# Scores of two chunks back to back in steps 3 to 5, x of step 3 transposed by TensorE, and the last output rows in two column parts

## The chip, the core and the metric

The kernel runs on one core of one Trainium2 chip. The metric is device time in microseconds (us) from launch to end, lower is better. Before the change the median of 5 runs is 200.76 us (200.41 to 204.0).

## What is computed

Gated linear attention over 4 batches, 8 heads, 768 positions and head dimension 48, followed by a feed-forward block with a ReLU gate on the 3072 resulting rows of 384 columns:

```python
f = sigmoid(f_logit)
for t in range(S):
    state = f[:, :, t, :, None] * state + k[:, :, t] outer v[:, :, t]
    y[:, :, t] = q[:, :, t] @ state
x = y.transpose(0, 2, 1, 3).reshape(B * S, H * D)
out = (relu(x @ w_gate) * (x @ w_val)) @ w_out      # 384 -> 1536 -> 384
```

Inputs and output are float32; the kernel multiplies in bfloat16 and accumulates in float32.

## The kernel before

The sequence is cut into 6 steps (`c` = 0 to 5) of 128 positions. In each step there is one *chunk* per batch (`b` = 0 to 3), so 24 chunks, numbered `w = c * 4 + b`. For a chunk, ScalarE turns the forget gate into logarithms, TensorE adds them up over the positions (L580) and ScalarE makes the factors `expo` from them (L589, L591). GpSimd multiplies k and q with these factors into `hats` (L600, L603) and casts v into `vpad` (L556). The transposed q and k are in `qkT`: in steps 1 and 2 TensorE transposes them (L613, the copy at L619), from step 3 on a DMA through the transposing crossbar does it (L622, issued by SyncE). *Scores* are k·q for every pair of positions in the chunk, for 8 heads: eight matmuls (L636) with only 48 of the array's 128 rows in use, alternating between rows 0 to 47 and rows 64 to 111, into two PSUM banks `sA` and `sB`. VectorE multiplies each bank with the causal mask into `ptm` (L642). Then TensorE makes y from the old state (L671) and from `ptm` and `vpad` (L675), ScalarE copies y to `xn` (L689), and `xn` is transposed into `xT`: by TensorE and a VectorE copy (L697, L701) while `c < first_xbar_x`, else by a crossbar DMA issued by SyncE (L705). For the next step, TensorE multiplies `hats` with `vpad` (L716), VectorE adds the old state (L730), GpSimd multiplies with the decay (L732).

The feed-forward block of a step follows its chunks: `ffn_hidden` makes, for each of 12 blocks of 128 hidden columns, a gate product and a value product, three matmuls each (L748), ReLU on ScalarE (L755), gate times value on VectorE into `gT` (L759). Steps 0 and 1 do so for two chunks at a time (256 columns), the later ones for all four (512 columns). `ffn_out` multiplies `gT` with `w_out`, 12 matmuls of 384 columns for each chunk (L770), ScalarE copies the rows to `osb` (L782), SyncE stores them (L785). The output products of one step are spread over the hidden products of the next.

All instructions are recorded first and then put in order by a small planner, `Plan`: each has an engine, what it reads and writes, an assumed duration `occ`, a latency `lat` and a priority. The planner gives each engine one fixed order; at run time every engine works through its order and waits on semaphores. So a changed duration or limit moves instructions all over the kernel. PSUM has 8 banks, which the planner hands out; `Plan`'s limits say how many each kind of tile may hold: here `s` (scores) 2, `f` (feed-forward) 4, and 1 each for `y`, `kv`, `bc`, `tp` (a transposed tile) and `w`. Loads, crossbar transposes and stores are all issued by SyncE, in one fixed order; a load of step `c + 1` or later (L397) also waits until the load three before it has landed. The weights are loaded from GpSimd's queue (L417). Until the first hidden product of step 0 TensorE is kept running by matmuls on zeros (L453), which the planner drops from there on.

The last rows stored are those of chunk 3 of step 5: 12 matmuls, one copy, one store.

Of the kernel before, what the change touches and what calls it, by code (L numbers as in the profile page):

```python
# [5 lines left out]
AF = mybir.ActivationFunctionType  # L6
# [37 lines left out]
class Plan:  # L44
# [184 lines left out]
def bass_hgrn2_outer__then__ffn_reglu_kernel(  # L229
# [21 lines left out]
    spread_engines = ['ACT', 'DVE', 'ACT', 'ACT']  # L251
    load_engine = 'SP'
    n_tiled = 1
    first_xbar_x = 3
    load_batches = 2
    hat_engines = ['DVE', 'POOL']
    groups = [(0,0,4,1),(1,0,2,0),(1,2,4,0),(2,0,4,0),(3,0,4,0),(4,0,4,0),(5,0,4,0)]
    B, H, S, D = q.shape
    C = 128
    NC = S // C  # L260
    HD = H * D
    DM, DFF = w_gate.shape
    NK = HD // 128
    NJ = DFF // 128
# [11 lines left out]
    bneg = [sb(f"bneg{i}", [128, 2, H, 64], BF16) for i in range(NB)]  # L276
# [5 lines left out]
    qkT_all = sb("qkT", [128, NQ, 2, NP, C], BF16)  # L282
    qkT = [qkT_all[:, i, :, :, :] for i in range(NQ)]
    NM = 3
    ptm = [sb(f"ptm{i}", [128, 2, NP, C], BF16) for i in range(NM)]
    NV = 4
    vpad = [sb(f"vpad{i}", [128, VW], BF16) for i in range(NV)]
# [18 lines left out]
    osb = [sb(f"osb{i}", [128, DM], F32) for i in range(NO)]  # L306
    tri = sb("tri", [128, C], BF16)
# [4 lines left out]
    zeros = sb("zeros", [128, 256], BF16)  # L312
    ident = sb("ident", [128, 128], BF16)
    ones = sb("ones", [128, 1], BF16)
    banks = [nc.alloc_psum_tensor(f"ps{i}", [128, 512], F32) for i in range(8)]

    pl = Plan({"bc": 1, "tp": 1, "s": 2, "y": 1, "kv": 1, "f": 4, "w": 1})
    pl.settled, pl.margin = 40.0, {"PE": 0.5, "SP": 0.6}
    add = pl.add
    gp, ve, sc, te, sy = nc.gpsimd, nc.vector, nc.scalar, nc.tensor, nc.sync  # L320

    def pe_t(*cols):
        return sum(max(n, 64) / 2400.0 + 0.0025 for n in cols)

    PE_L = 0.30

    def act_t(n):
        return dict(occ=0.06 + n / 1200.0, lat=0.25)
# [24 lines left out]
        ["ident"], ["ident"], occ=0.3, prio=-8)  # L353
    add("POOL", lambda: gp.memset(ones[:], 1.0), [], ["ones"], occ=0.1, prio=-8)

    def zero(eng, e, t, name, cols, prio):
        add(eng, lambda: e.memzero(t), [], [name], occ=0.15 + cols / 2000.0, prio=prio)  # L357

    zero("DVE", ve, zeros[:], "zeros", 128, -20)
    for i in range(NB):  # L360
        zero("DVE", ve, bneg[i][:], f"bneg{i}", 1024, -9)
    for i in range(NH):
# [41 lines left out]
    WJ = NJ // wsteps  # L404
# [21 lines left out]
    for item in early:  # L426
# [17 lines left out]
    def chain(line, *args, **kw):  # L444

        last = tails.get(line)
        tails[line] = add(*args, follows=[last] if last else [], **kw)
        return tails[line]
# [3 lines left out]
    for i in range(NWARM):  # L452
        op = add("PE", lambda: te.matmul(cold.ap[:, 0:256], zeros[:, 0:128], zeros[:, :]), ["zeros"], [cold], occ=0.22 if i < 17 else 0.11,  # L453
                 lat=PE_L, prio=1000000, opens=[cold] if i == 0 else [])
# [3 lines left out]
    def first_pair(pr):  # L458
        P = pr * 20
        bs = (2 * pr, 2 * pr + 1)  # L460
# [83 lines left out]
    def attention(c, b):  # L544
        w = c * B + b
        P = w * 10
        li = c % NL
        bi, bj = (w // 2) % NB, w % 2
        ei, hi, qi, mi, vi, ai = w % NE, w % NH, w % NQ, w % NM, w % NV, w % NA
        xi = c % NX  # L550
        fin, kin, qin, vin = (ld[n][li] for n in "fkqv")

        qk_key = [f"qkT{qi}_0", f"qkT{qi}_1"]
# [3 lines left out]
            prio=P + 3, occ=0.15 + HD / 1200.0 * 1.1, lat=0.2)  # L557
# [7 lines left out]
        else:  # L565
            parts = [(b, b + 2)] if b % 2 == 0 else []
# [9 lines left out]
            bn = bneg[bi][:, bj, :, :]  # L576
            bc = Bank("bc")

            def cum():
# [2 lines left out]
                    mm = te.matmul(bc.ap[:, HD + p:HD + p + 1],  # L582
                                   bn[:, 2 * p:2 * p + 2, :].rearrange("p h d -> p (h d)"), ones[:, :])
                return mm
            chain("cum", "PE", cum, ["tri", "ones", f"bneg{bi}", f"bn{bi}_{bj}"], [bc], occ=0.48, lat=PE_L,
                prio=P, opens=[bc])

            ex = expo[ei]
# [17 lines left out]
            if c < first_xbar_qk:  # L606
                tp = Bank("tp")

                def transposes():
# [7 lines left out]
                    opens=[tp])  # L617
# [12 lines left out]
        sA, sB = Bank("s"), Bank("s")  # L630

        def scores():
# [3 lines left out]
                    mm = te.matmul(s.ap[:, p * C:(p + 1) * C], qkT[qi][lo:lo + D, 1, p, :],  # L636
                                   qkT[qi][lo:lo + D, 0, p, :])
            return mm
        chain("scores", "PE", scores, qk_key, [sA, sB], occ=0.36, lat=PE_L, prio=P + 5, opens=[sA, sB])
        mask = tri[:].unsqueeze(1).to_broadcast([128, NP, C])  # L640
        for j, s in ((0, sA), (1, sB)):
            add("DVE", lambda j=j, s=s: ve.tensor_tensor(  # L642
# [3 lines left out]
        y = Bank("y")  # L646
# [38 lines left out]
        else:  # L685
# [5 lines left out]
            if c < first_xbar_x:  # L691
# [3 lines left out]
                def transpose_x():  # L695
                    for kt in range(NK):
# [3 lines left out]
                      opens=[xp])  # L700
# [3 lines left out]
            else:  # L704
                op = add("SP", lambda: sy.dma_start(xT[xi][:, :, b * C:(b + 1) * C], xn[ni][:, :], transpose=True),  # L705
                         [f"xn{ni}"], x_key, prio=P + 8, occ=1.2, lat=1.2)
# [3 lines left out]
        if c < NC - 1:  # L710
            kv = Bank("kv")
            s_new = st[b][c % 2]

            def state():
# [6 lines left out]
                occ=pe_t(96, 96, 96, 96), lat=PE_L, prio=P + 6 if c else 50 + b, opens=[kv])  # L721
# [6 lines left out]
            else:  # L728
# [3 lines left out]
                add("POOL", lambda: gp.tensor_tensor(t4(s_new), t4(tmp), rate, ALU.mult),  # L732
                    [key] + dk, [f"S{b}_{c % 2}"], prio=P + 8, **pool_t(HD))


    def ffn_hidden(c, b0, b1, j):
        xi, gi, ri = c % NX, c % NG, (count["h"]) % NR
# [24 lines left out]
    def ffn_out(g, *bs):  # L762

        gi = g % NG
        outs = [Bank("f") for b in bs]

        def proj_out(o, b, s):
            def run():
                for j in range(s * OJ, (s + 1) * OJ):
                    mm = te.matmul(o.ap[:, 0:DM], gT[gi][:, j, b * C:(b + 1) * C], wo[:, j, :],  # L770
                                   start=(j == 0), stop=(j == NJ - 1))
                return mm
            return run
        for s in range(NJ // OJ):
            js = range(s * OJ, (s + 1) * OJ)
            for o, b in zip(outs, bs):
                P = (g + 1) * B * 10 + 5 + NJ * 3 + b * 3
                chain("ffn", "PE", proj_out(o, b, s), [f"gT{gi}_{j}_{b}" for j in js] + sorted({f"wo{j // WJ}" for j in js}),
                      [o], occ=pe_t(*[DM] * OJ), lat=PE_L, prio=P + 1000, opens=[o] if s == 0 else [])
        for o, b in zip(outs, bs):  # L780
            oi, P = (g * B + b) % NO, (g + 1) * B * 10 + 5 + NJ * 3 + b * 3
            add("ACT", lambda o=o, oi=oi: sc.activation(osb[oi][:, :], o.ap[:, 0:DM], AF.Copy), [o], [f"osb{oi}"],  # L782
                prio=P, **act_t(DM))
            dst = bass.AP(tensor=out.tensor, offset=(b * S + g * C) * DM, ap=[[DM, C], [1, DM]])
            op = add("SP", lambda dst=dst, oi=oi: sy.dma_start(dst, osb[oi][:, :]), [f"osb{oi}"], [f"out{g}_{b}"],  # L785
                     occ=0.2, lat=0.9, prio=P)
            dma(op, f"osb{oi}", 0.45)

    OJ = 4
    OPAIR = 2  # L790
# [5 lines left out]
    for c in range(NC):  # L796
        for b in range(0, B, load_batches):
            for n in "fkqv":
                if c > max(int(x.split(".")[0]) for x in sent):
                    if load_engine == "SP":  # L800
                        loads.append(load(n, c, b, b + load_batches, loads[-flight:][:1]))
                    else:
                        loads.append(load(n, c, b, b + load_batches, paced=loads[-flight:][:1], eng="ACT"))
        for b in range(B):
            attention(c, b)
        if c == 0 and split_first:
            for s in range(wsteps):
                for b0 in (0, 2):
                    for j in range(s * WJ, (s + 1) * WJ):
                        ffn_hidden(0, b0, b0 + 2, j)  # L810
            for b in range(0, B, OPAIR):
                ffn_out(0, *range(b, b + OPAIR))
        for gc, b0, b1, now in groups:
            if gc != c or (c == 0 and split_first):
                continue
            for j in range(NJ):
                ffn_hidden(c, b0, b1, j)
                if pend and (NJ - 1 - j) * 1.0 / NJ * len0 < len(pend):
                    ffn_out(*pend.pop(0))
# [11 lines left out]
    for e in ("PE", "ACT", "DVE", "POOL"):  # L831
        n = 0
# [72 lines left out]
```

## Time and profile before

| | |
|---|---|
| median of 5 runs | 200.76 us |
| the profiled execution | 200.41 us, of which the span of the instructions is 198.7 us |
| VectorE / ScalarE / GpSimd busy | 107.3 / 115.1 / 77.2 us of the span |
| TensorE clock granted | full speed throughout |
| matmuls of the feed-forward block (L748, L770) | 125.0 and 52.2 us by the page |
| scores (L636) | 192 matmuls in 24 groups of 8 |
| crossbar transposes of x (L705) | 12, of which 4 in step 3 |

TensorE's row in the page is its matmul time; matmuls overlap each other in the pipeline, so the duration of one (say 326 ns) is longer than the time after which the next one starts. Where the text speaks of a *cadence*, it is the time from one group's start to the next group's start in the timeline, divided by the matmuls in the group.

### The profile page before, as it was taken

Reading aid. Unit: us, or ns where it says so; the run is one execution under the profiler, and the core shown is the slowest. Engines: PE = TensorE matmul, PEld = TensorE weight load, DVE = VectorE, ACT = ScalarE, POOL = GpSimd, SP = SyncE. Lnnn points to the kernel's source line nnn. Section 1 sums busy time; section 2 is a strip of 40 time slices with the busy share of each in tenths; the row PEclk is TensorE's granted clock in tenths of the full one; section 3 lists DMA queues with packets and bytes.
Section 4 is the critical chain, followed back from the end, with each engine's and each line's share of the span. In section 5 each row is a group of like instructions: output and inputs, shape, how many; then the busy total and the mean of one; then the engine's idle time right before and its main releaser. Section 6 shows DMA issues by size and latency. Waiting matters only on the chain.

```text
span 198.7 us, 4530 instructions
## 1 busy us (share of the span) xinstructions
PE 192.1 (97%) x1796; PEld 122.8 (62%) x1796; DVE 107.3 (54%) x208; ACT 115.1 (58%) x263; POOL 77.2 (39%) x111
## 2 busy tenths in 40 slices
PE   7999999999999999999998979999999999999994
PEld 5877688856888787755553535555555555544552
DVE  7268865564399877648737443636265233443300
ACT  2786767906788587876759466386425334344311
POOL 5198303823859677693564174504500000000000
PEclk9999999999999999999999999999999999999999
DMA  5999999999999999999997899989942200111112
GB/s 122 236 226 206 188 212 191 205 206 242 262 200 230 187 241 217 147 228 216 159 193 158 175 186 202 206 189 185 182 112 59 63 35 5 40 40 43 40 71 87
DMA packets 118180, 31.74 MB, mean 160 GB/s; under 512 B 111248, under 2 KB 118160, under 8 KB 118160
## 3 DMA queue, kind: packets, MB, share of 16 engines
q1 hardware_dynamic: 114176, 27.93, 71.4%
q0 software_dynamic: 3984, 3.54, 11.2%
q8 instruction: 14, 0.23, 0.5%
q14 instruction: 6, 0.05, 0.1%
HBM read 25.95 MB, written 4.72 MB: 154 GB/s over the span
## 4 chain that ended last, share of the span: by engine, by line
PE 67%; DMA 17%; SPq 9%; ACT 3%; POOL 2%; issue 1%
PE ps L748 35%; PE ps L770 21%; DMA v_in<-in_v_dram 9%; SPq L397 8%; DMA wv<-in_moe_w_val_dram 3%; PE ps L636 3%; DMA q_in<-in_q_dram 3%; DMA f_in<-in_f_logit_dram 2%; PE ps L675 2%; PE ps L613 2%; PE ps L671 1%; PE ps L716 1%; ACT relu L755 1%; PE ps L580 1%; POOL hats L603 1%; POOL vpad L556 1%
## 5 line engine op out<-in xcount | busy, mean ns | idle before, releaser
L759 DVE TENSOR_TENSOR gT<-relu,ps 128x256 bf16<-128x256 bf16 (+1 forms) x96 | 52.2, 552 | 58.4 <-PE ps L748 40.2
L748 PE MATMUL ps<-xT,wv 128*128 128x256 bf16 (+1 forms) x288 | 62.5, 326 | 0.2 <-DMA wv<-in_moe_w_val_dram 0.2
L748 PE MATMUL ps<-xT,wg 128*128 128x256 bf16 (+1 forms) x288 | 62.5, 326 | 0.1
L755 ACT ACTIVATE relu<-ps 128x256 bf16<-128x256 f32 (+1 forms) x96 | 46.0, 489 | 27.2 <-PE ps L748 26.9
L770 PE MATMUL ps<-wo,gT 128*128 128x384 bf16 x288 | 52.2, 326 | 0.0
L770 PEld LDWEIGHTS ps<-wo,gT 128*128 128x128 bf16 x288 | 26.6, 97 | 16.8
L748 PEld LDWEIGHTS ps<-xT,wv 128*128 128x128 bf16 x288 | 26.1, 97 | 16.4 <-DMA wv<-in_moe_w_val_dram 0.4
L642 DVE TENSOR_TENSOR ptm<-ps,tri 128x512 bf16<-128x512 f32 x48 | 31.0, 685 | 9.5 <-PE ps L636 9.4
L748 PEld LDWEIGHTS ps<-xT,wg 128*128 128x128 bf16 x288 | 26.6, 98 | 15.1 <-DMA xT<-xn 0.8
L782 ACT ACTIVATE osb<-ps 128x384 f32<-128x384 f32 x24 | 11.7, 491 | 32.4 <-PE ps L770 32.4
L600 POOL TENSOR_TENSOR hats<-k_in,expo 128x384 bf16<-128x384 f32 x20 | 20.0, 998 | 17.1 <-ACT expo L589 17.1
L603 POOL TENSOR_TENSOR hats<-q_in,expo 128x384 bf16<-128x384 f32 x20 | 19.8, 998 | 11.0 <-DMA q_in<-in_q_dram 9.7
L732 POOL TENSOR_TENSOR st<-ssum,dec 128x384 bf16<-128x384 f32 x16 | 13.2, 828 | 12.9 <-DVE ssum L730 12.9
L453 PE MATMUL ps<-zeros 128*128 128x256 bf16 x96 | 14.1, 305 | 1.1 <-DVE zeros L357 1.1
L556 POOL CAST vpad<-v_in 128x384 bf16<-128x384 f32 x24 | 12.2, 524 | 4.7 <-DMA v_in<-in_v_dram 4.7
L689 ACT ACTIVATE xn<-ps 128x384 bf16<-128x384 f32 x20 | 9.8, 490 | 6.0 <-PE ps L675 6.0
L589 ACT ACTIVATE expo<-ps 128x384 f32<-128x384 f32 x20 | 9.8, 490 | 3.9 <-PE ps L582 3.7
L453 PEld LDWEIGHTS ps<-zeros 128*128 128x128 bf16 x96 | 10.0, 109 | 3.1 <-DVE zeros L357 1.1
L570 ACT ACTIVATE f_in<-f_in 128x768 f32<-128x768 f32 x10 | 8.4, 838 | 4.3 <-DMA f_in<-in_f_logit_dram 4.3
L730 DVE TENSOR_TENSOR ssum<-ps,st 128x384 f32<-128x384 f32 x16 | 8.8, 552 | 3.5 <-PE ps L716 3.5
L636 PE MATMUL ps<-qkT 48*128 48x128 bf16 x192 | 9.5, 219 | 0.5 <-DMA qkT<-hats 0.5
L591 ACT ACTIVATE expo<-ps 128x384 f32<-128x384 f32 x20 | 9.9, 495 | 0.0
(71 smaller groups left out, 153.8 us busy)
## 6 DMA issues: line engine op xcount, KB each, us to landing
out_dram<-osb SPq DMA_DIRECT2D x24, 192.0 KB, 2.2
f_in<-in_f_logit_dram SPq DMA_DIRECT2D x10, 384.0 KB, 5.7
k_in<-in_k_dram SPq DMA_DIRECT2D x10, 384.0 KB, 5.4
q_in<-in_q_dram SPq DMA_DIRECT2D x10, 384.0 KB, 5.1
v_in<-in_v_dram SPq DMA_DIRECT2D x10, 384.0 KB, 5.2
wg<-in_moe_w_gate_dram POOLq DMA_DIRECT2D x3, 384.0 KB, 7.1
wv<-in_moe_w_val_dram POOLq DMA_DIRECT2D x3, 384.0 KB, 7.0
wo<-in_moe_w_out_dram POOLq DMA_DIRECT2D x3, 384.0 KB, 7.3
```

What stands on the lines that cost most here:

```text
L397: op = add(eng, lambda: e.dma_start(dst, src), [], [f"{n}{c % NL}_{b}" for b in range(b0, b1)], occ=(0.8 if eng == "SP" else 0.3) * (b1 - ...
L453: op = add("PE", lambda: te.matmul(cold.ap[:, 0:256], zeros[:, 0:128], zeros[:, :]), ["zeros"], [cold], occ=0.22 if i < 17 else 0.11, lat= ...
L556: add("POOL", lambda: gp.tensor_copy(vout, vin[:, b, :, :].rearrange("p (n j) d -> p n j d", j=2)), [f"v{li}_{b}", f"vpad{vi}"], [f"v_{vi} ...
L600: add("POOL", lambda: gp.tensor_tensor(hk, kin[:, b, :, :], ex[:, 1, :].rearrange("p (h d) -> p h d", h=H), ALU.mult), [f"k{li}_{b}", f"ex ...
L603: add("POOL", lambda: gp.tensor_tensor(hq, qin[:, b, :, :], ex[:, 0, :].rearrange("p (h d) -> p h d", h=H), ALU.mult), [f"q{li}_{b}", f"ex ...
L636: mm = te.matmul(s.ap[:, p * C:(p + 1) * C], qkT[qi][lo:lo + D, 1, p, :], qkT[qi][lo:lo + D, 0, p, :])
L642: add("DVE", lambda j=j, s=s: ve.tensor_tensor(ptm[mi][:, j, :, :], s.ap[:, :].rearrange("p (n t) -> p n t", n=NP), mask, ALU.mult), [s, " ...
L732: add("POOL", lambda: gp.tensor_tensor(t4(s_new), t4(tmp), rate, ALU.mult), [key] + dk, [f"S{b}_{c % 2}"], prio=P + 8, **pool_t(HD))
L748: mm = te.matmul(bank.ap[:, 0:n], wt[:, kt, j * 128:(j + 1) * 128], xT[xi][:, kt, n0:n1], start=(kt == 0), stop=(kt == NK - 1))
L755: add("ACT", lambda: sc.activation(relu[ri][:, 0:n], gate.ap[:, 0:n], AF.Relu), [gate], [f"relu{ri}"], prio=P, **act_t(n))
L759: add("DVE", lambda: ve.tensor_tensor(gT[gi][:, j, n0:n1], relu[ri][:, 0:n], val.ap[:, 0:n], ALU.mult), [val, f"relu{ri}"], [f"gT{gi}_{j}_ ...
L770: mm = te.matmul(o.ap[:, 0:DM], gT[gi][:, j, b * C:(b + 1) * C], wo[:, j, :], start=(j == 0), stop=(j == NJ - 1))
```

## The change

Four things are edited, and the planner then makes a new order for every engine:

- In steps 3 to 5 (`PAIR`) the chunks are handled two at a time by a new function `attend`: the scores of both chunks are one entry in TensorE's order, 16 matmuls, which opens four PSUM banks at once. The limit of `s` goes from 2 to 4, for all steps.
- `first_xbar_x` goes from 3 to 4: x of step 3 is transposed by TensorE and copied by VectorE; the four crossbar transposes of that step are no longer issued.
- The last chunk's output rows are made, copied and stored as columns 0 to 255 and columns 256 to 383, one part after the other, each with its own PSUM bank.
- Two assumed times of the planner: a sum over positions in steps 1 to 5 counts 0.29 us in place of 0.48, and the clearing of `zeros` gets a latency of 0.9 us.

```diff
-    first_xbar_x = 3
+    first_xbar_x = 4
+    TAIL = [0, 256, 384]
+    PAIR = [1, 1, 1, 2, 2, 2]
-    pl = Plan({"bc": 1, "tp": 1, "s": 2, "y": 1, "kv": 1, "f": 4, "w": 1})
+    pl = Plan({"bc": 1, "tp": 1, "s": 4, "y": 1, "kv": 1, "f": 4, "w": 1})
...
-    zero("DVE", ve, zeros[:], "zeros", 128, -20)
+    zero("DVE", ve, zeros[:], "zeros", 128, -20, 0.9)
...
-            chain("cum", "PE", cum, [...], [bc], occ=0.48, lat=PE_L,
+            chain("cum", "PE", cum, [...], [bc], occ=0.29, lat=PE_L,
...
-        chain("scores", "PE", scores, qk_key, [sA, sB], occ=0.36, lat=PE_L, prio=P + 5, opens=[sA, sB])
+        yield P, qk_key, scores, [sA, sB]
...
+    def attend(c, bs):
+        works = [attention(c, b) for b in bs]
+        heads = [next(x) for x in works]
+        def scores():
+            for h in heads:
+                mm = h[2]()
+            return mm
+        sbanks = [x for h in heads for x in h[3]]
+        chain("scores", "PE", scores, [x for h in heads for x in h[1]], sbanks, occ=0.2 + 0.22 * len(heads), lat=PE_L,
+              prio=heads[0][0] + 5, opens=sbanks)
+        for x in works:
+            for _ in x:
+                pass
...
-        for b in range(B):
-            attention(c, b)
+        n = PAIR[c]
+        for b in range(0, B, n):
+            attend(c, range(b, b + n))
...
     def ffn_out(g, *bs):
-        outs = [Bank("f") for b in bs]
+        cuts = TAIL if (g, bs[-1]) == (NC - 1, B - 1) else [0, DM]
+        parts = [(b, n0, n1, Bank("f")) for b in bs for n0, n1 in zip(cuts, cuts[1:])]
...
-                    mm = te.matmul(o.ap[:, 0:DM], gT[gi][:, j, b * C:(b + 1) * C], wo[:, j, :],
+                    mm = te.matmul(o.ap[:, 0:n1 - n0], gT[gi][:, j, b * C:(b + 1) * C], wo[:, j, n0:n1],
...
+        if len(cuts) > 2:
+            for part in parts:
+                for s in range(NJ // OJ):
+                    rows(*part, s)
```

In the new order TensorE has these differences that the next part needs. Up to the multiplication for the next state of the first chunk of step 1 (the first one of L716 with `hats`) it stands 12 output products behind the 48 hidden ones, and not 16. In step 0 the fourth transposition of `hats` and the scores and back-transpositions of chunks 2 and 3 all stand before the first value product; before, the scores of chunk 3 stood behind it. On SyncE, the loads of f and k for the second half of step 4 stand before the crossbar transposes of that step's first chunk, the q load directly behind the first of these, the v load behind the second.

More of the change, by code (lines that the diff above doesn't have):

```diff
@@ L354, in bass_hgrn2_outer__then__ffn_reglu_kernel, with zero @@
     add("POOL", lambda: gp.memset(ones[:], 1.0), [], ["ones"], occ=0.1, prio=-8)
-    def zero(eng, e, t, name, cols, prio):
-        add(eng, lambda: e.memzero(t), [], [name], occ=0.15 + cols / 2000.0, prio=prio)
-    zero("DVE", ve, zeros[:], "zeros", 128, -20)
+    def zero(eng, e, t, name, cols, prio, lat=0.2):
+        add(eng, lambda: e.memzero(t), [], [name], occ=0.15 + cols / 2000.0, lat=lat, prio=prio)
+    zero("DVE", ve, zeros[:], "zeros", 128, -20, 0.9)
     for i in range(NB):
@@ L584, in cum @@
                 return mm
-            chain("cum", "PE", cum, ["tri", "ones", f"bneg{bi}", f"bn{bi}_{bj}"], [bc], occ=0.48, lat=PE_L,
+            chain("cum", "PE", cum, ["tri", "ones", f"bneg{bi}", f"bn{bi}_{bj}"], [bc], occ=0.29, lat=PE_L,
                 prio=P, opens=[bc])
@@ L764, in ffn_out, with proj_out @@
         gi = g % NG
-        outs = [Bank("f") for b in bs]
-        def proj_out(o, b, s):
+        cuts = TAIL if (g, bs[-1]) == (NC - 1, B - 1) else [0, DM]
+        parts = [(b, n0, n1, Bank("f")) for b in bs for n0, n1 in zip(cuts, cuts[1:])]
+        def proj_out(o, b, s, n0, n1):
             def run():
                 for j in range(s * OJ, (s + 1) * OJ):
-                    mm = te.matmul(o.ap[:, 0:DM], gT[gi][:, j, b * C:(b + 1) * C], wo[:, j, :],
+                    mm = te.matmul(o.ap[:, 0:n1 - n0], gT[gi][:, j, b * C:(b + 1) * C], wo[:, j, n0:n1],
                                    start=(j == 0), stop=(j == NJ - 1))
@@ L773, in proj_out, with rows @@
             return run
-        for s in range(NJ // OJ):
+        def rows(b, n0, n1, o, s):
             js = range(s * OJ, (s + 1) * OJ)
[L776 to L780, printed above, removed]
+            P = (g + 1) * B * 10 + 5 + NJ * 3 + b * 3
+            chain("ffn", "PE", proj_out(o, b, s, n0, n1), [f"gT{gi}_{j}_{b}" for j in js] + sorted({f"wo{j // WJ}" for j in js}),
+                  [o], occ=pe_t(*[n1 - n0] * OJ), lat=PE_L, prio=P + 1000, opens=[o] if s == 0 else [])
+        if len(cuts) > 2:
+            for part in parts:
+                for s in range(NJ // OJ):
+                    rows(*part, s)
+        else:
+            for s in range(NJ // OJ):
+                for part in parts:
+                    rows(*part, s)
+        for b, n0, n1, o in parts:
             oi, P = (g * B + b) % NO, (g + 1) * B * 10 + 5 + NJ * 3 + b * 3
[L782 to L785, printed above, removed]
+            add("ACT", lambda o=o, oi=oi, n0=n0, n1=n1: sc.activation(osb[oi][:, n0:n1], o.ap[:, 0:n1 - n0], AF.Copy), [o], [f"osb{oi}_{x}" for x in TAIL[:-1] if n0 <= x < n1],
+                prio=P, **act_t(n1 - n0))
+            dst = bass.AP(tensor=out.tensor, offset=(b * S + g * C) * DM + n0, ap=[[DM, C], [1, n1 - n0]])
+            op = add("SP", lambda dst=dst, oi=oi, n0=n0, n1=n1: sy.dma_start(dst, osb[oi][:, n0:n1]), [f"osb{oi}_{x}" for x in TAIL[:-1] if n0 <= x < n1], [f"out{g}_{b}_{n0}"],
                      occ=0.2, lat=0.9, prio=P)
-            dma(op, f"osb{oi}", 0.45)
+            dma(op, f"osb{oi}_{n0}", 0.45 * (n1 - n0) / DM)
     OJ = 4
```

## The prediction

> **What bounds the kernel now.** I read the page's busy shares first, then TensorE's waits, then its timeline around each wait, then SyncE's timeline there.
>
> ```profile
> PE 192.1 (97%) x1796; PEld 122.8 (62%) x1796; DVE 107.3 (54%) x208; ACT 115.1 (58%) x263; POOL 77.2 (39%) x111
> ```
>
> TensorE is busy for 192.1 of 198.7 us; no other engine passes 58%. So there are only two ways to gain: less TensorE time, or fewer of its stalls. Its own waits:
>
> ```profile
> PE ps L716 <- POOL vpad L556: 1.6, 2, 1.1
> PE ps L453 <- DVE zeros L357: 1.1, 1, 1.1
> PE ps L636 <- DMA qkT<-hats: 0.5, 1, 0.5
> PE ps L580 <- ACT bneg L573: 0.2, 1, 0.2
> PE ps L748 <- DMA wv<-in_moe_w_val_dram: 0.2, 1, 0.2
> ```
>
> None is for a PSUM bank. L716 waits twice: 0.48 us at 43.88 and 1.11 us at 115.94. The first ends with a landing: v of step 1, issued at 31.39, lands at 43.27, is cast, and L716 starts at 43.88. Nothing in TensorE's order moves that moment, so I call it **the pin** and count work from there. The second, in the chain of waits:
>
> ```profile
> 107.87 0.37 SPq L705
> 108.24 0.05 issue
> 108.29 5.14 DMA q_in<-in_q_dram
> 113.43 0.07 issue
> 113.50 1.95 POOL hats L603 x2
> 115.44 0.46 POOL vpad L556
> ```
>
> A load of q for step 4 is issued only at 108.29, behind a crossbar transpose of x of step 3 (L705), and GpSimd and TensorE wait for it. The same happens ten microseconds earlier: the f load leaves at 98.38, behind a transpose that held SyncE from 95.38 to 98.34, and the wait on bneg at 105.35 follows. **SyncE's queue is what makes the late stalls.**
>
> Cadences in the timeline show more than the waits: where a group took longer from start to next start than its like does elsewhere. L748 x3 (512 columns) takes 0.65; at 114.03 it took 1.92 (+1.27), at 107.62 before scores 1.27 in place of 0.74 (+0.53), at 104.34 1.01 (+0.37), at 138.34 0.81 (+0.17); scores at 108.90 took 0.49 in place of 0.33 (+0.16). Sum 2.50 us, all between 104 and 139.
>
> **Scores in pairs.** The timeline around one group:
>
> ```profile
> 122.01 0.81 PE L748 MATMUL ps<-xT,wv 128*128 128x512 bf16 x3
> 122.66 0.81 PE L748 MATMUL ps<-xT,wg 128*128 128x512 bf16 x3
> 123.40 0.40 PE L636 MATMUL ps<-qkT 48*128 48x128 bf16 x8
> 123.73 0.61 PE L748 MATMUL ps<-xT,wv 128*128 128x512 bf16 x2
> ```
>
> From 122.66 to 123.40 is 0.74, not 0.65: 0.09 on entering the 48-row form. The eight then take 0.33. They run in pairs (the starts lie at 0, 66, 122 and 177 ns), one pair each 0.056, which is also the cadence of a 128-column transpose (L613, 8 in 0.446). So four pairs need 0.22 and 0.11 goes on leaving. One group costs 0.42, two 0.84. Sixteen in a row do not occur in this trace: between no gain (0.84) and one entry and exit (0.09 + 8 x 0.056 + 0.11 = 0.65). I take 0.65, since pairs inside a group show no such cost. Six times 0.20 saved: **-1.19 us**, between 0 and -1.2. The price is banks: four of eight are held until VectorE has done four maskings (L642, 0.685 each: 2.74 us) where it was 1.37. The Trainium skill warns of just this (TensorEngine Tiling (Array Packing), "Gotcha 1: PSUM Pressure" and "PSUM Bottleneck": row tiles need banks of their own, and emptying PSUM may become the bound). By that rule the pair would hand its gain back; by the rows VectorE is busy 14.3 of 30 us between 120 and 150, and no wait on a bank shows. I go by the rows and keep the rule for a rival.
>
> **x of step 3 on TensorE.** Added are 4 x 3 transposes. L697's cadence is 0.166 for 3, next to feed-forward matmuls without a switching cost: 4 x 0.166 = **+0.67**. The Trainium skill prices a TensorE transpose at about 275 ns in a kernel (TensorE: Matmul & The Clock Gate, "Part 4: PE-mode transpose"), which gives 3.3 us and would make this edit a loss. The row has 219 ns for one from start to end, but 56 ns to the next start, and it is the next start that a full TensorE pays; the rule's figure is a latency. I take 0.67. Four copies of 0.352 (L701) go to VectorE, +1.4 us beside 16 idle us between 80 and 120: nothing on the path; uncovered they would cost 0.35 each at the first hidden product of step 4. ScalarE's copies to xn (L689) stay.
>
> Removed from SyncE are four transposes, at 92.40 (2.31), 95.38 (2.96), 103.74 (1.25) and 106.99 (1.25), 7.8 us of its queue with their waits on xn. What stood behind them moves up. f and k of step 4's second half go before the transposes of its first chunk, which start when `hats` is done (98.65); q follows at about 101 (a transpose holds the queue for 1.3 to 3.5), and with the 5.1 us of that load lands at 106. TensorE reaches L716 of that chunk at about 111 in the new order. Before it GpSimd needs two q products, one k product and the cast, 1.0 + 1.0 + 1.0 + 0.5 = 3.5: ready at 109.5. Slack some 1.5 us where there was a wait of 1.1. So the 2.50 should go. Next late would be the second crossbar transpose of a chunk pair, for a pair of scores now waits for both; by the same reckoning it lands at about 105 to 106 against scores at 109. New waits of the fresh order I allow **0.4**, between 0 and 2: among them the start of step 2, where a transposition, the multiplication for the next state, x and scores stand with only one hidden product between, and the 0.685 copy at L619 may come 0.2 late. Together **-2.1**.
>
> **The start.** In step 0 more stands before the first value product: transposition (0.45), ScalarE's two spreads (0.68 each, L526), then scores. In place of 21.71 (the landing of wv) I put it at about 22.8. The new order has 4 output products fewer before the pin (4 x 0.1625 = 0.65), and there were 0.48 of waiting: it still arrives at about 43.4, the pin stays at 43.9. But those four products come after it: **+0.65**. Bounds: if v lands earlier, up to -0.5; if the start is another 0.5 late, hardly anything. Fewer zero matmuls cost and bring nothing, the loads lead there.
>
> **The tail.** The last copy has 128 columns: 256 cost 0.383 (L755), 384 cost 0.49 (L782), so 0.28, 0.21 less. The first part's copy and store lie beside the 12 matmuls of the second (0.67). SyncE needs about 0.6 from issue to issue and has 0.57: nothing. The last store keeps its 1.86 from issue to landing (196.34 to 198.20). The split itself: 256 columns 0.109, 128 columns 0.056, together 0.0024 over one of 384, times 12 = 0.03. **-0.2**, between +0.1 and -0.4.
>
> **Sum.** -1.19 + 0.67 - 2.1 + 0.65 - 0.2 = -2.17, about **-2.1**. The profiled execution, 200.41 (span 198.70 and 1.71 around it), becomes 198.3; it is 0.35 below the median of the runs, so the median of 200.76 becomes **198.6**.
>
> **Rivals.** *The queue stays late.* Crossbar transposes of q and k still stand between the loads, and with each pair of scores waiting for two of them, half of the 2.5 us remains or comes back as waits on `qkT`. For it: one of the old waits was of this kind, and the slack at 111 hangs on how long a transpose holds SyncE (1.3 to 3.5). Against: f, k and q all leave several us sooner. Time: 198.6 + 1.25 = 199.9.
>
> *The start decides.* The first value product comes later than I put it and TensorE misses the pin by 0.5, while pairs save only half: 198.6 + 0.5 + 0.6 = 199.7. For it: ScalarE's spreads are in line. Against: 0.5 of slack, and the measured gap in the 48-row form.
>
> *Banks (the slower side).* Place: the six pairs of scores. With y, kv and bc open, one to three banks are left to the feed-forward; after about two products of 0.65 TensorE must wait until VectorE, behind four maskings, has multiplied gate by value (0.686). Price: up to 2.74 + 0.69 - 1.3 = 2.1 per pair, and it decides from 2.1/6 = 0.35 per pair. At 0.7 per pair: 198.6 + 4.2 = 202.8. For it: 2.74 us of maskings in one piece. Against: the new order puts a gate-by-value product between maskings in step 4, has attention work of 0.2 to 0.4 between the products, and today's scores with two banks cause no wait on a bank at all.
>
> **Chances.** A measurement of this kernel tells about 0.3% from no change, 0.6 us. Forecast 0.66 (198.6, own range 197.7 to 199.4), queue 0.17, start 0.07, banks 0.10. Faster by over 0.3% means below 200.15: the forecast, most of queue and start, 0.85; same 0.06; slower 0.09. The range runs from 197.7 (no new waits, an earlier pin) to 200.2, the upper end of the queue's case.
>
> **What would show it.** In the profile after: scores x16 taking about 0.55 to the next start, TensorE's waits on bneg, on vpad at 115 and on qkT gone, the q load of step 4's second half issued before 103, L697 x36, the first value product at about 22.8 and L716 still at 43.9, the last copy 0.28. Wrong would be new TensorE waits on VectorE or ScalarE within 3 us after scores (banks), 16 scores taking over 0.7 (no saving in pairs), or L716 later than 44.4 (start).

## The result, and the profile after

The changed kernel takes 200.72 us (median of 43 runs, 198.98 to 203.75) where the kernel before takes 201.30 (80 runs on the same chips): a ratio of 0.9966, 95% interval 0.9951 to 0.9981. The ratio leaves out the executions of either kernel that ran over 1.5% longer than its fastest, some of them at a lower granted clock. The change is faster by 0.3% and outside the predicted range of 197.7 to 200.2. The profiled run of the changed kernel took 200.72 us too, with a span of 199.0; before's took 200.41 with 198.7. So the two profiles differ by +0.3 us, while the medians differ by -0.6: the profiled run of before was a lucky one, 0.9 under what became its median.

Two views of the changed kernel, the page's row of busy times and TensorE's longest waits (line, what it waited for, us in total, times, longest):

```profile
PE 190.9 (96%) x1813; PEld 123.7 (62%) x1813; DVE 106.9 (54%) x212; ACT 114.8 (58%) x264; POOL 77.5 (39%) x111
```

```profile
PE ps L582 <- ACT bneg L575: 2.3, 2, 2.1
PE ps L455 <- DVE zeros L359: 1.1, 1, 1.1
PE ps L518 <- DVE hats L508: 0.9, 1, 0.9
PE ps L638 <- ACT qkT L528: 0.8, 1, 0.8
PE ps L718 <- POOL vpad L558: 0.3, 1, 0.3
```

TensorE has 1.2 us less busy time. That is not the pairs' 1.19 alone: 7 fewer matmuls on zeros are in it (13.1 us for 14.1) and 12 more transposes. The waits on `vpad` at 116 and on `qkT` are gone. One wait of 2.1 us that did not exist has come: L582, the running sums, waits for `bneg`. (Two shorter new ones, on `hats` at 11.67 and on `qkT` at 21.51, lie in the start, where TensorE still waits for v afterwards.) The timeline of TensorE around it (start, duration, instruction, and in brackets the idle time before it with what ended it):

```profile
125.97 0.81 PE L789 MATMUL ps<-wo,gT 128*128 128x384 bf16 x4
128.89 0.34 PE L582 MATMUL ps<-bneg,tri 128*128 128x384 bf16 x1 [2.10 <-ACT bneg L575]
129.06 0.24 PE L584 MATMUL ps<-ones,bneg 128*128 128x1 bf16 x4
129.16 1.46 PE L789 MATMUL ps<-wo,gT 128*128 128x384 bf16 x8
```

The chain of waits leads back from there to SyncE's queue (start, duration, what):

```profile
118.98 0.69 SPq L812
119.67 0.04 issue
119.71 1.20 SPq L707
120.91 0.04 issue
120.95 5.42 DMA f_in<-in_f_logit_dram
126.37 0.02 issue
126.39 0.84 ACT f_in L572
127.24 0.38 ACT xn L691
127.61 0.49 ACT relu L773
128.10 0.74 ACT bneg L575
128.84 0.05 issue
128.89 0.34 PE ps L582
```

Read it upwards: the sums wait for `bneg`, ScalarE makes `bneg` 2.5 us after the f load of step 5's second half has landed, and that load left only at 120.95, behind a store (L812) and a crossbar transpose of x of step 4 (L707). It is the mechanism that the prediction saw in step 4, one step later. Before, the same load left at 123.21 and landed at 129.99, and TensorE came to these sums at 132.69, without a wait:

```profile
123.21 1.97 SPq L397 DMA_DIRECT2D f_in<-in_f_logit_dram  x1
132.69 0.33 PE L580 MATMUL ps<-bneg,tri 128*128 128x384 bf16 x1
```

Now the load lands 3.6 us earlier, but TensorE comes to the sums at 126.79, 5.9 us earlier. Most of that is a new place in the order, not a faster TensorE: between the pin (the start of L718 with `hats`) and these sums stand 114 matmuls of hidden products with 512 columns where 132 stood before, 18 fewer at 0.216 each, 3.9 us. The pairs are not needed for it: in the kernel `x_alone` below, which has none, TensorE comes to the sums 82.5 us after the pin, in the changed kernel 82.7, before 88.8.

An account of the two profiled runs, from the start of L718 (the pin) to the start of the last group of output products, 187.82 before and 188.64 after. "Work" is a count: what stands behind the pin, times the cadences of the prediction. "Waits" is the rest:

| | before | after | difference |
|---|---|---|---|
| the pin | 43.88 | 44.08 | +0.20 |
| work behind it | 141.32 | 141.45 | +0.13 |
| waits behind it | 2.62 | 3.10 | +0.48 |
| from that group to the end of the span | 10.88 | 10.36 | -0.52 |
| sum | 198.7 | 199.0 | +0.3 |

By the count the work changes by -1.19 for the pairs, +0.67 for x and +0.65 for four output products that moved behind the pin, together +0.13. The trace bears out the cadences in it: all six groups of sixteen scores take 0.55 to the next start, and the group ahead of them 0.74 instead of 0.65, the 0.09 of entering. The first of the six:

```profile
88.65 0.81 PE L766 MATMUL ps<-xT,wg 128*128 128x512 bf16 x3
89.39 0.62 PE L638 MATMUL ps<-qkT 48*128 48x128 bf16 x16
89.94 0.82 PE L766 MATMUL ps<-xT,wv 128*128 128x512 bf16 x3
```

What did not come is the 2.1 us of vanished stalls.

### The profile page after: what moved, and what is told of

Same layout as the page of the kernel before. It is cut to its first block, busy times and chain, and to the rows that moved or that the text cites. A ratio compares the mean times of both kernels' runs of the same rounds, so it can differ in the third digit from the quotient of the medians.

```text
span 199.0 us, 4570 instructions
## 1 busy us (share of the span) xinstructions
PE 190.9 (96%) x1813; PEld 123.7 (62%) x1813; DVE 106.9 (54%) x212; ACT 114.8 (58%) x264; POOL 77.5 (39%) x111
## 4 chain that ended last, share of the span: by engine, by line
PE 61%; DMA 18%; SPq 11%; ACT 3%; POOL 3%; issue 1%; DVE 0%
PE ps L766 31%; PE ps L789 19%; SPq L399 9%; DMA v_in<-in_v_dram 8%; DMA f_in<-in_f_logit_dram 6%; DMA wv<-in_moe_w_val_dram 4%; PE ps L638 2%; PE ps L615 2%; PE ps L582 1%; SPq L624 1%; PE ps L677 1%; PE ps L673 1%; PE ps L718 1%; POOL vpad L558 1%; POOL hats L605 1%
## 5 line engine op out<-in xcount | busy, mean ns | idle before, releaser
L789 PE MATMUL ps<-wo,gT 128*128 128x384 bf16 (+2 forms) x300 | 52.4, 320 | 0.1
L789 PEld LDWEIGHTS ps<-wo,gT 128*128 128x128 bf16 x300 | 27.6, 98 | 17.8 <-DMA wo<-in_moe_w_out_dram 0.5
L809 ACT ACTIVATE osb<-ps 128x384 f32<-128x384 f32 (+2 forms) x25 | 11.8, 476 | 30.0 <-PE ps L789 30.0
L455 PE MATMUL ps<-zeros 128*128 128x256 bf16 x89 | 13.1, 303 | 1.1 <-DVE zeros L359 1.1
L455 PEld LDWEIGHTS ps<-zeros 128*128 128x128 bf16 x89 | 9.1, 109 | 3.0 <-DVE zeros L359 1.1
L638 PE MATMUL ps<-qkT 48*128 48x128 bf16 x192 | 8.5, 218 | 0.9 <-ACT qkT L528 0.8
```

The costliest lines, as they stand in the source:

```text
L789: mm = te.matmul(o.ap[:, 0:n1 - n0], gT[gi][:, j, b * C:(b + 1) * C], wo[:, j, n0:n1], start=(j == 0), stop=(j == NJ - 1))
```

## Experiments

All kernels below are the changed kernel, or the one before, with the edit shown (its main lines). Every ratio is to the kernel before on the same chip. The theory: SyncE's queue sets the late waits, the change brings TensorE to its next need earlier by more than it brings the load earlier, and so the waits move from step 4 to step 5. The first rival: the DMA engines are full, and the order on SyncE matters little. The second: the pairs themselves cost what they save.

### The f load sent earlier, and the sums planned later

`f_front` changes only SyncE's order, `late_f` only the time that the planner assumes for the landing:

```
 order = pl.schedule([bk for bk in banks])
+sp = order["SP"]        # f_front: the f load of step 5's second half
+sp.remove(early)        # directly behind the v load of its first half
+sp.insert(sp.index(ahead) + 1, early)

-(6.0 if (c, n, b0) == (1, "v", 0) else 2.0)                       # late_f
+{(1, "v", 0): 6.0, (5, "f", 2): 5.5}.get((c, n, b0), 2.0)
```

> The changed kernel with one thing different: in SyncE's order the f load of step 5's second half stands directly behind the v load of its first half, ahead of the store of row block (2, 0) and of the crossbar transpose of x of step 4. All other engines keep their order. Queue theory (the load is late because it stands behind these two): it is issued at about 118 in place of 121 and lands at about 123.5 in place of 126.4, TensorE's wait on bneg in step 5 falls from 2.1 to under 0.3 us, ratio to before about 0.987. Throughput theory (the DMA engines are full and deliver no sooner whatever the order): it lands within 0.7 us of 126.4, the wait stays over 1.3 us, ratio about 0.995.

> The changed kernel, with the planner told that the f load of step 5's second half lands 3.5 us later than it assumed; so the sums of step 5's second half stand some 3.3 us of TensorE work later in the order. Queue and throughput theory alike: the load lands when it did, but TensorE has other work until then; the wait of 2.1 us falls under 0.5, ratio about 0.987 to 0.989. If the time that the wait costs is lost in any order (work behind it is late for other reasons too), waits of 1.5 us or more show up elsewhere and the ratio stays at 0.995 or above.

Measured: `f_front` 0.9933 (0.9906 to 0.9960), `late_f` 0.9931 (0.9901 to 0.9962), each some 0.7 us better than the changed kernel by the ratios, though the intervals overlap with its own (0.9951 to 0.9981), and short of the 0.987 that was expected. In `f_front` the load left at 118.2 and landed at 123.4, where full DMA engines would have had it land at about 126.4, and the 2.1 us are gone. But the next one in the queue is late:

```profile
PE ps L718 <- POOL vpad L558: 1.6, 1, 1.6
PE ps L638 <- DMA qkT<-hats: 1.3, 1, 1.3
```

These are TensorE's two longest waits in `f_front`. The wait on `qkT` lies at 131, before the first pair of scores of step 5, whose two transpositions were issued at 125.7 and 127.8. (The one on `vpad` is the pin, at 45.0 in this run.) `late_f` has the same wait, 1.2 us, at the same place. So the late load is the cause of the wait on the sums, its place in the queue is what made it late, and the queue has a second item late behind the first.

### One part alone

`pairs_alone` is the kernel before with the pairs, `x_alone` with the x of step 3 on TensorE, `tail_alone` with the split of the last rows:

```
-PAIR = [1] * 6            pairs_alone, with "s": 4 for "s": 2
+PAIR = [1, 1, 1, 2, 2, 2]
-first_xbar_x = 3          x_alone
+first_xbar_x = 4
-TAIL = [0, 384]           tail_alone
+TAIL = [0, 256, 384]
```

> The kernel before with only the pairs of scores (limit of s at 4); x of step 3 by crossbar, one tail part, old assumed times. If a pair saves 0.20 us as the cadence of the single groups says: 16 scores take 0.55 to the next start, TensorE's work is 1.2 us less; with waits on loads no worse than before (2.5 us) the ratio is 0.993 to 0.995. If four banks cost waits (bank rival): TensorE waits on VectorE or ScalarE of over 0.35 us behind pairs, ratio over 1.000. If the new order waits more on loads, waits on bneg, vpad or qkT of over 3 us, ratio 0.998 or more.

> The kernel before with only x of step 3 transposed by TensorE. TensorE's work is 0.67 us more. If the four crossbar transposes were what made the loads of step 4 and 5 late: the 2.5 us of waits between 104 and 139 go, ratio 0.991 to 0.993. If TensorE's order moves ahead by as much as the loads do, so that waits on loads return one step later (what the changed kernel's profile shows): waits on bneg, vpad or qkT of 1.5 us or more remain, ratio 0.999 to 1.003.

> The kernel before with only the last output rows in two column parts. The trace of the changed kernel has the last copy 0.21 shorter and its last store landing 1.54 instead of 1.86 after issue: together 0.5 us, ratio 0.9975 (0.996 to 0.999), and the same two numbers in this run's trace. Rival, the prediction's own term of 0.2 us (the store keeps its 1.86): 0.999 and no difference in the landing.

`pairs_alone`: 1.0222 (1.0179 to 1.0266). The pairs take 0.55 as in the changed kernel, and with four output products moved behind the pin here too the work behind it is 0.54 us less (140.78), and yet the kernel is 2.2% slower: the waits behind the pin are 6.5 us. TensorE's waits of 0.5 us and more:

```profile
PE ps L718 <- POOL vpad L558: 2.1, 2, 1.4
PE ps L582 <- ACT bneg L575: 2.0, 2, 1.7
PE ps L638 <- DMA qkT<-hats: 1.3, 1, 1.3
PE ps L455 <- DVE zeros L359: 1.1, 1, 1.1
PE ps L638 <- ACT qkT L528: 0.8, 1, 0.8
PE ps L638 <- DVE gT L777: 0.5, 1, 0.5
PE ps L766 <- DMA xT<-xn: 0.5, 1, 0.5
```

Everything that comes over SyncE is late: `vpad` (v), `bneg` (f), `qkT`, `xT`. The line that names `gT` looks like a wait for a bank, but that `gT` was done at 138.47, and the scores started at 138.83, 0.09 after the crossbar transposition of their `qkT` had landed (138.74): it is one more wait for the queue. Pairs on a queue that also carries the transposes of step 3 are a loss. Banks, which the prediction called the price of the pairs, are not what they cost here. The limit of `s` is raised in this kernel too; the pairs were not run without it.

`x_alone`: 1.0016 (0.9992 to 1.0039), no difference that can be told from none. The 0.67 us of work buys 0.9 us fewer waits behind the pin (2.62 to 1.76): those at 104 to 116 mostly go, and one of 0.9 on `bneg` comes at 128.7. In this run the pin was late, at 45.34, and TensorE with it; an earlier pin would have made that wait longer.

`tail_alone`: 1.0000 (0.9973 to 1.0027). In its trace the part from the last output group to the end is 10.36 where it was 10.88, the 0.5 us that was expected, and the last store lands 1.54 after its issue; the time cannot confirm it, since the expected 0.9975 lies just inside the interval. The run is useful for something else. Its program is before's up to the last rows, but in the profiled run (202.19 us) the f load of step 5's second half landed at 131.9 instead of 129.99, and the waits behind the pin came to 4.6 us instead of 2.6. So late waits of what is up to there one program differ by 2 us between two runs, and before's profile has the lower of the two. The fourth part of the change, the two assumed times, was in no run alone.

### Step 4's x on TensorE as well

```
-first_xbar_x = 4
+first_xbar_x = 5
```

> The changed kernel with the x of step 4 transposed by TensorE too (first_xbar_x = 5): no crossbar transpose of x stands between the loads of step 5, and TensorE has 0.67 us more work. If the transposes of x ahead of the f load of step 5's second half are the whole cause of the 2.1 us wait: the f load is issued at 119.7 or earlier and lands by 125, the wait is below 0.5, ratio about 0.992. Rival, the planned order asks for the sums of that half earlier than any queue brings them (its order on TensorE moves them up by another 1.5 us because the plan sees the queue empty): a wait of 2 us on bneg stays, ratio about 1.000.

Measured: 1.0038 (1.0009 to 1.0066), slower than before. No transpose of x stands ahead of the f load of step 5's second half, and still:

```profile
PE ps L615 <- POOL hats L605: 1.8, 1, 1.8
PE ps L582 <- ACT bneg L575: 1.7, 1, 1.7
```

The f load was issued at 121.8, even later than in the changed kernel, because everything ahead of it was. The wait on `bneg` is still 1.7. So the crossbar transposes of x are not the whole cause: the fixed order on TensorE asks for the sums before the queue, with or without them, can have brought f. (The wait on `hats` is in the start and differs from run to run. TensorE's transposes of x also brought a wait of their own, 1.0 us on `xn` at 117.8.)

### The whole stretch of the queue put in order of need

`qkt_front` sends f, k and the two `qkT` transpositions of step 5's first pair ahead of step 4's store and x; `q_front` also the q load behind them:

```
+behind("v2_0", "f2_2", "k2_2", "qkT2_0", "qkT3_0")                    # qkt_front
+behind("v2_0", "f2_2", "k2_2", "qkT2_0", "qkT3_0", "q2_2",            # q_front
+       "out2_0_0", "xT0_0", "xT0_1", "v2_2")
```

> The changed kernel with SyncE's order alone changed: behind the v load of step 5's first half now come at once the f load and the k load of its second half and the two transpositions to qkT for its first pair of scores; the output store and the two x transposes of step 4 that stood between come after them. Nothing else moves. Queue theory: f is issued at about 118 and landed by 123.5, the two qkT transpositions are issued at about 121.5 and 122.5 and landed by 126.5, so both the wait of 2.1 us on bneg and the 1.3 us on qkT that f_front got in its place go; at least 2 of the 3.1 us of excess behind the pin go, ratio to before 0.987 (0.985 to 0.990). Rival, the DMA engines are full and a new order only decides who is late: a wait of 1.2 us or more comes back on the x of step 4, on q or on v, and the ratio stays at 0.993 like f_front.

> The kernel qkt_front, and on SyncE also the q load of step 5's second half directly behind the two qkT transpositions of its first pair (ahead of the store and the first x transposes of step 4), and the v load ahead of the other x transposes. In qkt_front a wait of 1.0 us was left at 141, for the two qkT transpositions of the last pair of scores: their q load had left at 130.7 and landed at 134.8. Queue theory: q leaves at about 127, lands at about 131, the transpositions land at about 138, the wait is gone, and less than 0.9 us of waiting is left behind the pin: 0.6 to 1.0 us less than qkt_front, ratio to before 0.984 (0.980 to 0.988). Rival, the queue only hands the delay on: 0.8 us or more of new waits on the x of step 4 or on hats, ratio 0.988 or above.

`qkt_front`: 0.9880 (0.9819 to 0.9942). Both waits near 130 are gone; 1.0 us is left at 142, where the last pair of scores waits for its transpositions. `q_front`: **0.9866 (0.9824 to 0.9908)**, median 198.19, the best kernel of the study: 1.0% below the changed one. SyncE's timeline in it (the third column is the engine; x2 are two transpositions in a row):

```profile
118.14 0.58 SPq L399 DMA_DIRECT2D v_in<-in_v_dram  x1
118.77 1.69 SPq L399 DMA_DIRECT2D f_in<-in_f_logit_dram  x1
120.50 1.96 SPq L399 DMA_DIRECT2D k_in<-in_k_dram  x1
122.50 4.70 SPq L624 DMA_TRANSPOSE qkT<-hats  x2
127.26 0.57 SPq L399 DMA_DIRECT2D q_in<-in_q_dram  x1
127.87 1.53 SPq L812 DMA_DIRECT2D out_dram<-osb  x1
129.44 2.49 SPq L707 DMA_TRANSPOSE xT<-xn  x2
```

The store and the first transpose of x, which took 118.11 to 120.91 in the changed kernel, come after the loads, and nobody waits for them. The waits behind the pin are 1.0 us, against 3.1, while the work is the same (141.44 against 141.45). This is the clearest verdict on the theory: the same work, the same loads, a different order on one queue, 2 us fewer waits in the trace, and an interval that lies clear of the changed kernel's. The gain over `qkt_front` that was expected is within the intervals and not shown by the times. Nor is the wait of the last pair all gone, as was expected:

```profile
141.76 0.62 PE L638 MATMUL ps<-qkT 48*128 48x128 bf16 x16 [0.69 <-DVE gT L777]
```

Here too `gT` was done earlier (141.22), while the second transposition landed at 141.67, 0.09 ahead of the scores.

### What the pairs are worth

`no_pairs` is the changed kernel with single scores, `q_front_single` and `qkt_front_single` the two kernels above with single scores:

```
-PAIR = [1, 1, 1, 2, 2, 2]
+PAIR = [1] * 6              with "s": 2 and the planned 0.36 for single scores
```

> The changed kernel without the pairs of scores (x of step 3 on TensorE, the start and the tail stay). By the sum's first term alone it is 1.19 us slower than the changed kernel, ratio to before 1.0025. If the new wait of 2.1 us on the sums is what the pairs' order brings (a pair moves the work behind it forward, and the sums with it), that wait is mostly gone here and the ratio is 0.995 to 0.998, like the changed kernel; wait on bneg near 129 below 1 us.

> The kernel qkt_front without pairs: each chunk's scores stand alone again (PAIR all 1, two banks), with the same order on SyncE for step 5. If the pairs save what the sum said (0.20 each, six of them), TensorE has 1.19 us more work than in qkt_front and the ratio is 0.006 above it (0.993). Rival, the pairs give their gain back as waits (banks held by four maskings, two transpositions needed at once): within 0.002 of qkt_front or below it.

> The kernel q_front without pairs. With the late waits out of both kernels the pairs' own worth is seen: 1.19 us of TensorE time saved against what pairs wait for. The trace of qkt_front_single had 5 groups of output products ahead of the pin where the paired order has 3 (1.30 us) and a pin 1.1 us later, so the start counts for 0.2 at most. If the pairs' saving stands once the queue is early: 1.0 to 1.2 us above q_front (ratio 0.989 to 0.990). Rival, pairs are worth nothing because a pair waits for two transpositions and holds what follows: within 0.4 us of q_front.

| kernel | ratio | output products ahead of the pin | pin to last output group | work | waits |
|---|---|---|---|---|---|
| changed kernel | 0.9966 (0.9951 to 0.9981) | 12 | 144.55 | 141.45 | 3.10 |
| no_pairs | 0.9941 (0.9908 to 0.9973) | 20 | 142.82 | 141.33 | 1.49 |
| qkt_front | 0.9880 (0.9819 to 0.9942) | 12 | 143.67 | 141.45 | 2.2 |
| qkt_front_single | 0.9897 (0.9843 to 0.9951) | 20 | 142.20 | 141.33 | 0.9 |
| q_front | 0.9866 (0.9824 to 0.9908) | 12 | 142.45 | 141.44 | 1.01 |
| q_front_single | 0.9922 (0.9891 to 0.9953) | 20 | 142.18 | 141.33 | 0.85 |

Inside the change as it is, the pairs bring nothing that shows: without them the ratio is 0.9941 against 0.9966, with intervals that overlap, and the wait on the sums is 0.45 us where it was 2.10:

```profile
128.77 0.34 PE L582 MATMUL ps<-bneg,tri 128*128 128x384 bf16 x1 [0.45 <-ACT bneg L575]
```

The work column shows why it is not a loss of 1.19. A single-score order has 8 more output products ahead of the pin, 8 x 0.1625 = 1.30. Take that out and the column has the pairs at 141.33 + 1.30 - 141.44 = 1.19 us; it must, for it is a count with the prediction's cadences. What is measured is behind it: in `q_front` all six groups of sixteen take 0.55 to 0.56 to the next start, in `q_front_single` the groups of eight in these steps 0.33. So TensorE's time is saved, and in the changed kernel's profile it was paid back in two ways: as waits (3.10 against 1.49), and by a start that puts 8 products behind the pin (the next part takes this one up).

What the pairs are worth in time once the queue is in order is not settled. The ratios of `q_front` and `q_front_single` lie 0.0056 apart, 1.1 us in favour of the pairs, as expected, but they are medians of 6 and 10 runs and their intervals overlap. In the two profiled runs the last output group starts at 187.81 and 187.87, no difference. And `qkt_front` and `qkt_front_single` lie 0.0017 apart where 0.006 was expected; that is the figure of the rival, that the pairs give their gain back.

### The start: who moved the output products

The limit on score banks was raised from two to four for all steps, although only steps 3 to 5 have pairs. `caps_occ` gives pairs their own limit; `caps_occ_q` adds SyncE's order of `q_front`:

```
-Plan({..., "s": 4, ...})
+Plan({..., "s": 2, "sp": 4, ...})
-sA, sB = Bank("s"), Bank("s")
+sA, sB = (Bank("s" if PAIR[c] == 1 else "sp") for _ in range(2))
-occ=0.2 + 0.22 * len(heads)
+occ=0.36 if len(heads) == 1 else 0.64
```

> The changed kernel with the planner's limit of four score banks kept to the pairs of steps 3 to 5; the single scores of steps 0 to 2 have two banks and the planned duration of 0.36 again, as in the kernel before. What is computed and all pairs stay. If the limit of four banks is what moved output products behind the pin, 20 products stand ahead of the pin (12 in the changed kernel, 16 before) and the work behind it is 1.30 us less than in the changed kernel (140.1 to the last group of output products); the late waits of some 3 us stay. Ratio 0.991 (0.988 to 0.994), against 0.9966. Rival, the start is bound by the landing of wo and v whatever the order: the pin moves 1.3 us later by waits on wo, ratio 0.996 to 0.998.

> The kernel caps_occ with SyncE's order of q_front. Both causes out: work behind the pin 140.1, waits behind it about 1.0 (as in q_front), last group of output products 141.2 after the pin. With the pin at 44.2 to 45.4 the ratio is 0.978 (0.974 to 0.982); it shows whether the two add up (q_front 0.9866). If the start is bound by the landings, no better than q_front.

Measured: `caps_occ` 0.9925 (0.9897 to 0.9952), as expected but not clear of the changed kernel, and `caps_occ_q` 0.9951 (0.9922 to 0.9979), far from the expected 0.978 and slower than `q_front`. In both 20 products stand ahead of the pin, and the work behind it is 140.15, 1.30 less. So the limit and the planned duration of a single score together moved the products; which of the two was not taken apart on the chip. What it buys is less: the pin comes at 45.06 and 44.78 instead of 44.08, with 0.8 to 0.9 us of waiting for wo, and the two gains do not add up: in `caps_occ_q` the waits behind the pin are 2.6 us, where `q_front` has 1.0. The longest:

```profile
PE ps L766 <- DMA xT<-xn: 1.2, 1, 1.2
```

TensorE has 1.3 us less to do ahead of step 5's first hidden products, so now the x transposes of step 4, which `q_front` could put last for nothing, are late: the wait is at 139.04. A queue's order that suits one order of TensorE need not suit another. One made for `caps_occ` was not tried.

## Why the prediction was wrong

**What failed: the late stalls, "So the 2.50 should go", and "New waits of the fresh order I allow 0.4".** The term was -2.1; the trace has +0.48. (Against the median of before rather than its fortunate profile it is nearer -0.4, an estimate: -0.6 between the medians, less the -0.19 of pin, work and tail in the account above, if these are what the two profiled runs had.) The loads of step 4 did what I said: q of its second half left at 102.99 instead of 108.29, and the waits at 104 to 116 all but vanished. But I followed the queue only to 113, where the stalls of before lay, and took the slack of the next stage for granted. There TensorE's new order comes to the sums 5.9 us earlier, 3.9 of it because the planner put 6 hidden products (18 matmuls) fewer ahead of them, and the f load lands only 3.6 us earlier. That is the mechanism of the rival *The queue stays late* (199.9), to which I gave 0.17; it let half of the 2.5 us come back, and I had placed its new waits on `qkT`. In the changed kernel the wait is on `bneg`; in `f_front` and `late_f`, with that wait taken away, one on `qkT` did appear.

**The pairs, -1.19: right as work, unproven as time.** Entry, cadence and exit are as worked out. That a pair waits for two transpositions I named, but I gave it slack by looking at step 4 only; in step 5 it cost 1.3 and 1.2 us in `f_front` and `late_f`. And what I put under the start, "4 output products fewer" against before, is 8 against single scores; `caps_occ` shows that the raised limit and the planned duration of a single score did that, not the pairs.

**x of step 3, +0.67: right.** Its four groups of three transposes take 0.16 to 0.18 to the next start (at 94.82, 97.56, 104.83 and 106.31), and the row was the better guide than the 275 ns of the Trainium skill (TensorE: Matmul & The Clock Gate, "Part 4: PE-mode transpose"), which would have made this 3.3 us: `x_alone` as a whole costs nothing measurable. What I left out is that this edit also moves the sums of step 5 forward in TensorE's order.

**The start, +0.65: right in size,** with the first value product at 22.73 (22.8 forecast). That the pin stays at 43.9 is true of the changed kernel's profile (44.08) but not in general: in `f_front`, `late_f`, `qkt_front` and `q_front`, which have the same order in the start, it lies at 45.01, 45.35, 44.46 and 45.36.

**The tail, -0.2: too small by 0.3.** The copy of 128 columns took 0.28, as forecast. But the last store did not keep its 1.86: issued at 196.97 it landed at 198.51, 1.54 later.

**Banks: did not happen at the scores.** In none of the nine kernels with pairs do the scores, or the products behind them, show a wait for a bank of over 0.2 us; the two lines that name `gT` ended with a landing of `qkT`. One wait for a bank is in them, 0.43 us at 116.29 in `qkt_front`: the sums wait until ScalarE has copied output rows out of theirs. "Gotcha 1: PSUM Pressure" of the Trainium skill (TensorEngine Tiling (Array Packing)) did not show as a wait at the scores here; raising the limit of banks did change the plan of the steps that have no pairs.

**From the profile to the median:** I put the profiled run 0.35 below the median of five. Over 80 runs it is 0.9. So against that fortunate profile the change shows +0.3, and against the median -0.6; a forecast that starts from the waits of one profiled run takes that run's luck along.

## What to carry to other kernels

When an edit makes a busy engine ask for its inputs sooner, be it by less work or by a new order, follow the queue that feeds it through every later stage: for each item, compare how much sooner the engine asks with how much sooner the item lands; the wait goes to the first one where the first number is larger. A queue that runs in a fixed order should carry loads ahead of stores and of transposes that have slack, and that order is valid for one order of the consumer only. A limit that is raised for one stage should be raised for that stage alone, or the plan of the others changes with it (here 8 output products in the start).

## What the runs showed of the hardware

- A store of 128 of 384 columns landed 1.54 us after its issue, the store of all 384 in 1.86.
- Entering and leaving the 48-row form costs 0.09 and 0.11 once, however many matmuls stand in between: sixteen took 0.64 with entering where two groups of eight had taken 0.84 together.
- On SyncE one crossbar transpose of x occupied the queue for 1.20 us where nothing held it up, and two of `qkT` in a row for 4.70 with their waits included; an ordinary load that was not held up took 0.58.
- The moment of the pin moved by 1.3 us (44.08 to 45.36) between kernels with the same order in the start, and the landing of one f load by 1.9 us between two runs with the same program ahead of it. What moved them was not looked for.
